# Attention followed by a feed-forward block: output stored by one DMA per token tile, under a new instruction order

## The chip, the cores and the metric

The kernel runs on one core of a Trainium2 chip. Its time is the device time of one execution in microseconds (us); the median of three runs is given. A profile is one further execution, recorded by the hardware profiler.

The core has five instruction streams that run side by side and meet at semaphores: PE (matrix multiplication, its weight loads shown as PEld), DVE (vector), ACT (activation functions), POOL (general purpose, here also the issuer of the loads from device memory) and SP (here only an issuer of DMAs). Each stream runs its own instructions strictly in program order. All DMAs of the core are carried by the same 16 DMA engines.

## The reference

A linear attention with an exponential feature map, and a feed-forward block behind it, without a residual:

```python
# q, k, v: (8 batches, 8 heads, 576 positions, 64); w_phi: (64, 128)
def phi(x):
    proj = einsum('bhsd,df->bhsf', x, w_phi)
    proj = proj - max(abs(proj), axis=-1, keepdims=True)
    return concatenate([exp(proj), exp(-proj)], axis=-1)
q_p, k_p = phi(q), phi(k)
kv = einsum('bhsf,bhsd->bhfd', k_p, v)
z  = sum(k_p, axis=2)
attn = einsum('bhsf,bhfd->bhsd', q_p, kv) / (einsum('bhsf,bhf->bhs', q_p, z) + 1e-6)
x = attn.transpose(0, 2, 1, 3).reshape(4608, 512)       # one row per token
h = maximum(x @ w_in, 0)                                # w_in (512, 2048)
out = (h * h) @ w_out                                   # w_out (2048, 512), float32
```

## The kernel before

The work falls into two halves that are laid over each other. The attention of the eight batches produces rows of x. The feed-forward block consumes them in 36 token tiles of 128 rows, four tiles to a chunk, nine chunks.

**Attention.** POOL issues the loads of k, v and q (line 350), which also turn them to bf16. From batch 2 on, SP issues transposing DMAs of k and q (line 419, tiles kT and qT); the first two batches are transposed by PE (line 430). PE multiplies by w_phi (lines 484, 625, 657), ACT takes exponentials (lines 513, 529, 632), PE forms kv (line 579) and the quotient's parts (line 725), DVE scales them into a tile xo of 128 tokens (line 746). Then xo is transposed into xT, for the later batches by a DMA that SP issues (line 765).

**Feed-forward.** `ffn_in` (line 777) multiplies xT by w_in (line 787), ACT takes the relu (line 792, tile hr), POOL or, from chunk 7 on, DVE squares it (lines 795 and 798, tile h). `ffn_out` (line 807) accumulates one token tile over 16 matmuls of 512 columns (line 818), in four parts of four. After the fourth part DVE copies the sum from PSUM to one of three buffers of 128 x 512 float32, the ring `r_ot` (tile ot, line 835), and SP stores it. A buffer is free again when its store has landed. The very last tile is done in two halves of 256 columns, each copied by its own engine and stored in two pieces, one issued by SP and one by ACT (line 830).

**Where rows lie.** A batch has 576 positions, which is nine blocks of 64 for each of the 64 places that line 804 calls p. So a token tile is two blocks, u = 0 and 1, on partitions 0 to 63 and 64 to 127 of ot. Block j of batch b goes to the rows b\*576 + 9\*p + j, so one block is 64 rows of 2 KB, nine rows apart. The order of the blocks in a batch is `jord` (lines 397 and 398), in pairs j and j + 2. Because nine is odd, four of the 36 tiles (4, 13, 22 and 31) hold the last block of one batch and the first of the next; all others lie in one batch.

**Order.** No scheduler runs in the kernel. Every piece of work is first recorded as an operation with a number, and `Plan.play` then emits the operations in the order of the long list `ORDER` (lines 93 to 184), which was found by a search outside the kernel. A negative number -n stands for n small matmuls that keep PE occupied (line 384). The rings give out their buffers in the order in which `ORDER` takes them. So the list settles the order on every engine and also which of the three ot buffers a tile gets. An SP issue carries a wait for the landing of the DMA that used the same of eight completion semaphores, which is the one eight issues back, beside the wait for its data.

Of the kernel before, what the change touches and what calls it, by code (L numbers as in the profile page):

```python
# [44 lines left out]
class Plan:  # L45
# [48 lines left out]
    7 9 11 6 13 15 17 19 10 1 2 8 4 5 -15 33 34 -3 50 54 51 16 -3 37 38 55 56 35 -1 72 39 52 36 57 59 53 73 74  # L94
    75 41 42 76 81 79 61 65 62 -6 94 40 -4 83 95 77 78 70 66 68 84 87 67 64 63 89 85 -2 43 44 18 -2 45 47 46 48
    -4 116 96 12 21 23 25 14 60 49 86 92 88 90 20 111 118 117 80 82 69 71 -1 100 102 58 91 115 114 97 93 27 29
    22 137 139 98 99 101 104 103 138 107 105 158 160 108 106 132 109 112 119 113 120 121 110 125 126 122 127
    159 133 136 135 134 140 128 153 154 161 157 179 123 129 124 141 142 146 147 130 131 155 156 181 143 144 148
    149 180 150 145 24 26 1465 1461 31 387 174 178 200 177 176 182 175 167 162 168 163 1462 169 164 1468 201
    170 165 171 202 1463 389 1466 1469 1470 1464 1467 166 183 214 215 151 216 188 184 189 152 195 198 199 197  # L100
    196 227 228 203 229 231 1471 185 190 218 186 1477 219 187 204 191 217 192 205 1472 1473 226 232 233 1478
    1474 1475 1476 1479 209 210 172 238 193 173 230 194 242 243 236 237 211 206 207 212 208 213 1480 239 244
    1481 247 1482 245 249 260 253 250 1494 1495 1490 256 257 246 240 1483 1486 241 234 1491 262 261 255 1487
    252 251 28 265 1508 30 220 222 267 221 223 224 225 266 235 1492 248 1489 1493 388 399 390 407 401 405 264
    258 254 259 1509 263 270 287 269 268 288 289 272 271 273 275 274 1510 1484 1496 391 393 1485 392 276 279
    278 303 306 305 277 308 309 310 304 280 281 290 307 32 1497 1501 1502 329 324 331 311 282 285 330 286 284
    283 1516 312 1504 1517 326 328 1505 327 325 332 394 1518 1506 1488 395 397 396 398 313 314 296 317 291 1507
    297 292 293 315 318 1511 316 298 299 300 294 400 1515 319 345 420 346 295 320 321 350 351 1519 301 347 322
    348 302 323 1498 1512 1522 349 1499 1513 1523 421 422 1520 1521 403 352 423 1526 1500 1514 402 371 373 372
    425 366 368 1527 353 1533 1525 354 1549 367 1534 369 1524 565 1535 567 1528 566 569 359 1532 333 427 426  # L110
    355 360 338 1529 1550 429 370 1530 424 428 1551 568 404 406 339 356 340 361 334 335 1539 362 341 363 357
    336 358 435 430 337 1536 374 1537 419 364 1546 365 342 437 436 1540 343 1541 344 438 439 571 1538 570 1531
    573 572 1555 1562 431 432 433 434 1547 1569 415 409 411 412 417 418 410 416 413 414 408 440 462 479 442 441
    443 1576 1577 1556 375 574 577 1548 589 579 583 1557 1573 464 376 380 1559 377 381 463 378 379 382 481 1558
    1542 480 483 482 1574 1560 1563 1564 444 484 383 384 486 485 575 0 1575 465 1561 487 446 447 453 445 506
    448 452 449 450 507 508 457 454 451 501 466 461 460 456 459 1552 1543 488 489 455 494 495 490 1553 458 1544
    576 591 593 509 1554 1579 504 1580 496 472 491 1566 385 492 497 473 498 493 467 474 468 475 476 1570 469
    470 471 503 502 745 1565 1581 747 1567 510 505 1571 386 1603 746 516 511 517 512 748 1503 499 477 580 603
    578 598 605 1585 513 518 514 519 515 520 521 604 1545 1589 1593 1597 1607 597 1572 1568 749 751 523 528 607
    526 524 1611 1615 600 599 601 527 529 530 1598 1616 581 582 478 500 522 1622 1623 1612 550 608 551 552 750  # L120
    752 602 525 1613 606 531 1624 753 1614 1600 1582 1630 609 610 1608 1601 1631 1583 553 755 1584 1632 585 586
    618 620 619 584 613 545 546 547 532 548 611 754 1609 612 1636 549 1637 1602 1610 1638 923 756 1640 1586
    1594 1595 554 1621 1587 1641 1642 1618 533 560 538 1625 590 592 587 1617 595 771 757 588 594 596 614 615
    1619 617 622 1596 925 1620 1588 621 534 539 555 684 1629 556 561 557 540 535 562 685 686 558 541 536 559
    542 1644 1633 563 564 537 1634 1604 1645 616 635 1605 924 662 663 664 636 639 637 638 758 630 631 632 624
    629 634 633 625 657 661 640 642 623 626 660 659 927 641 643 665 658 644 627 628 778 780 779 926 1639 1590
    650 1643 645 1591 666 687 929 928 1606 931 1592 646 651 679 728 730 1648 680 652 647 672 1647 653 729 731
    673 648 649 654 1651 769 1599 543 763 1578 761 775 759 667 674 1652 544 782 688 683 681 682 689 1626 1649
    1627 668 690 694 695 675 676 1675 696 691 669 670 692 671 693 697 698 1628 930 760 762 1679 706 701 783 708
    707 785 784 767 655 1683 705 703 704 702 781 1650 1646 1657 1661 1665 1687 709 710 786 723 726 724 764 788  # L130
    793 1688 1653 765 677 678 656 699 700 1669 794 1670 1676 1708 1694 727 787 1677 725 732 1695 1678 933 1712
    1662 1693 1697 770 776 772 773 774 1709 1710 1713 1663 777 795 789 790 791 792 766 768 820 815 798 822 1701
    821 738 739 800 799 1690 819 818 816 817 932 1103 1671 935 1635 1664 1696 1714 1691 1672 1720 1721 955 934
    953 797 1673 802 716 1666 717 740 741 711 733 718 712 734 1705 713 1706 719 714 735 1684 1658 801 736 742
    737 939 715 720 936 940 1674 1722 1692 1685 796 823 1659 1667 1668 1105 1660 1104 743 949 947 945 721 722
    951 937 1707 943 1689 812 806 842 843 844 804 805 803 808 807 809 810 811 813 837 838 814 840 841 839 956
    966 958 1654 1106 824 3 1655 1656 957 959 845 1107 1686 1109 1702 1680 1711 1715 830 1703 1681 846 968 831
    1719 825 826 832 847 852 848 853 833 967 1698 1704 1682 1699 1700 827 1723 849 854 1716 1717 1718 850 851
    828 855 856 834 1724 1729 970 1108 1733 859 860 908 829 938 1110 864 865 910 866 909 867 1111 1765 1769
    1773 863 862 861 868 969 881 886 887 961 884 885 744 835 857 941 836 858 1737 1741 963 888 1788 869 1744  # L140
    1742 874 1726 882 960 883 1745 1727 1113 889 1728 1738 962 964 875 870 876 1762 1739 1740 1763 911 1764
    1777 877 948 944 946 950 952 954 1020 976 1725 942 878 1021 978 1780 871 872 1022 873 1112 1789 890 1781
    965 1790 1746 1281 1730 1752 1747 1770 1753 1731 1114 1283 1782 1732 1778 977 980 971 903 906 907 972 973
    904 1771 912 1023 1754 1772 896 897 1784 1774 1751 1756 1775 905 974 1757 1758 918 891 892 1766 913 914 919
    1755 898 915 1785 1786 979 975 1767 1119 1117 1115 920 893 921 899 900 916 922 894 917 895 1743 879 1133
    1779 1127 1734 1759 1760 1116 1735 982 993 995 994 998 1000 999 1768 1001 984 981 983 996 1135 1736 1776
    997 1024 985 1002 986 988 990 1086 1087 1015 987 1016 1017 1018 989 1136 880 1783 1787 1791 991 992 1019
    1003 1025 1008 1748 1138 1137 1139 1749 1140 1026 1009 1030 1027 1801 1004 1031 1010 1032 1005 1006 1011
    1033 1028 1012 1007 1118 1795 1792 1793 1282 901 1131 1129 1120 1750 1805 1796 1034 1029 1088 1146 1147
    1042 1141 1142 1143 1044 1148 1013 1035 1121 1125 1123 1761 1809 1819 1823 1794 1827 902 1014 1036 1820  # L150
    1816 1810 1145 1821 1144 1043 1045 1817 1818 1811 1812 1822 1089 1284 1813 1814 1122 1150 1151 1064 1066
    1152 1059 1060 1061 1831 1832 1065 1153 1833 1842 1838 1824 1802 1062 1149 1063 1839 1843 1046 1825 1067
    1840 1285 1844 1826 1286 1124 1081 1085 1156 1037 1083 1038 1039 1041 1084 1068 1803 1040 1090 1157 1158
    1837 1841 1845 1860 1856 1861 1082 1857 1159 1804 1862 1287 1288 1047 1069 1070 1048 1834 1052 1071 1074
# [32 lines left out]
def kernel(  # L187
# [10 lines left out]
    nc = tc.nc  # L198
# [608 lines left out]
    def ffn_out(c, i, key):  # L807
# [25 lines left out]
        elif part == 3:  # L833
# [3 lines left out]
            def fn():  # L837
                for u in range(2):
                    g = 2 * (first[c] + tt) + u
                    nc.sync.dma_start(out=outv[g // NJ, jord[g // NJ % 2][g % NJ]],  # L840
                                      in_=o.t[u * 64 : u * 64 + 64, :])
# [88 lines left out]
```

## Time and profile before

| | before |
|---|---|
| median of 3 runs | 357.59 us (352.43, 357.59, 357.99) |
| the profiled execution | 352.77 us, its span 351.0 us |
| granted PE clock in the profile | 0.994 |
| PE busy | 339.3 us, 97% of the span |
| DVE / ACT / POOL busy | 243.6 / 242.6 / 197.9 us |
| DMA packets of the POOL queue (loads) | 16144, 18.35 MB, 35.3% of 16 engines' time |
| DMA packets of the SP queue (transposes, stores) | 50176, 20.00 MB, 34.5% |
| issues of stores of 128 KB | 70, median 2.4 us from issue to landing |

The span is the time from the first to the last instruction. Busy times are sums for an engine over the span. "SPq" is SP's issuing of DMAs, which is not counted as busy. A DMA's share is the time of its packets divided by the span of 16 engines; packets that overlap on one engine count twice. The three runs lie at two levels, one at 352.4 us and two near 357.8 us; the profiled execution stands with the lower.

### The profile page before, as it was taken

The numbers are of one execution on the slowest core, as the hardware profiler recorded it, in microseconds if no ns is written. First come the engines' busy times: TensorE is split into PE (matmuls) and PEld (weight loads), VectorE is DVE, ScalarE is ACT, GpSimd is POOL, SyncE is SP. The second block draws the span as 40 slices with busy tenths as digits, with TensorE's granted clock in tenths as the row PEclk, the third lists the DMA queues.
The fourth block names the chain that finished last, engine by engine and source line by source line (L and its number), as shares of the span: only waits on it lengthen the run. The fifth ranks groups of instructions, "written<-read, shape, count | busy, mean of one in ns | idle before, by whom it ended". The sixth has DMA issues, their size and how long they took to land.

```text
span 351.0 us, 10160 instructions
## 1 busy us (share of the span) xinstructions
PE 339.3 (97%) x4045; PEld 197.8 (56%) x4045; DVE 243.6 (69%) x553; ACT 242.6 (69%) x496; POOL 197.9 (56%) x305
## 2 busy tenths in 40 slices
PE   6999999998999999999999999998999999999995
PEld 3579877767645654465446544654545544544444
DVE  1999968995887898677867797667468446632531
ACT  3999997988588958895778649946795255703510
POOL 8865976859958672989397619945961020000000
PEclk9899999999999999999999999999999999999999
DMA  7999986998996995949996255793322323021134
GB/s 117 202 210 209 206 119 95 137 190 102 153 156 98 173 175 79 151 56 177 177 120 126 33 83 96 114 163 63 69 43 47 77 48 76 3 45 43 36 87 104
DMA packets 66528, 39.13 MB, mean 111 GB/s; under 512 B 46257, under 2 KB 60977, under 8 KB 66481
## 3 DMA queue, kind: packets, MB, share of 16 engines
q0 software_dynamic: 16144, 18.35, 35.3%
q1 hardware_dynamic: 50176, 20.00, 34.5%
q8 instruction: 31, 0.51, 0.6%
q10 hardware_dynamic: 160, 0.13, 0.2%
q14 instruction: 17, 0.13, 0.1%
HBM read 36.77 MB, written 9.44 MB: 132 GB/s over the span
## 4 chain that ended last, share of the span: by engine, by line
PE 85%; ACT 6%; DMA 4%; DVE 2%; issue 1%; SPq 0%; POOL 0%; DVEq 0%; POOLq 0%
PE one L787 35%; PE one L818 33%; PE one L725 5%; PE one L579 4%; PE one L484 2%; PE one L625 2%; PE one L657 2%; DMA xk<-in_k_dram 2%; ACT qph L632 2%; DMA xT<-xo 1%; ACT kph L529 1%; ACT kph L513 1%; ACT hr L792 1%; DVE mk L495 1%; DMA out_dram<-ot 1%
## 5 line engine op out<-in xcount | busy, mean ns | idle before, releaser
L795 POOL TENSOR_TENSOR h<-hr 128x512 bf16<-128x512 bf16 x112 | 114.3, 1039 | 52.2 <-ACT hr L792 48.1
L787 PE MATMUL one<-xT,win 128*128 128x512 bf16 (+2 forms) x768 | 138.5, 326 | 2.5 <-DVE xo L746 1.2
L818 PE MATMUL one<-wout,h 128*128 128x512 bf16 (+1 forms) x592 | 136.8, 373 | 0.0
L792 ACT ACTIVATE hr<-one 128x512 bf16<-128x512 f32 x144 | 84.7, 616 | 48.5 <-PE one L787 37.3
L787 PEld LDWEIGHTS <-win 128*128 128x128 bf16 x768 | 66.1, 98 | 51.4 <-issue 4.3
L632 ACT ACTIVATE qph<-one 128x512 bf16<-128x512 f32 (+1 forms) x160 | 81.1, 577 | 19.7 <-PE one L625 19.5
L818 PEld LDWEIGHTS <-h 128*128 128x128 bf16 x592 | 54.0, 98 | 56.2 <-issue 1.3
L513 ACT ACTIVATE kph<-ksh 128x1024 bf16<-128x1024 f32 (+1 forms) x66 | 62.1, 969 | 15.8 <-DVE ksh L505 15.7
L495 DVE TENSOR_REDUCE mk<-one 128x4 f32<-128x512 f32 (+1 forms) x80 | 49.6, 627 | 9.7 <-PE one L484 8.1
L687 POOL COPY mq<-m 64x4 f32<-64x4 f32 x108 | 20.0, 185 | 46.6 <-DVE m L678 42.8
L678 DVE TENSOR_REDUCE m<-one 128x4 f32<-128x512 f32 (+1 forms) x60 | 36.0, 630 | 13.9 <-PE one L657 10.4
L735 DVE TENSOR_TENSOR one<-one,em 128x260 f32<-128x260 f32 (+1 forms) x80 | 32.1, 430 | 19.0 <-PE one L725 14.2
L505 DVE TENSOR_TENSOR ksh<-one,mk 128x512 f32<-128x512 f32 (+1 forms) x66 | 41.4, 627 | 4.7 <-ACT kph L513 1.4
L725 PEld LDWEIGHTS <-qph 128*128 128x128 bf16 x640 | 30.9, 97 | 16.8 <-issue 0.9
L835 DVE COPY ot<-one 128x512 f32<-128x512 f32 x35 | 23.9, 684 | 18.5 <-PE one L818 18.3
L725 PE MATMUL one<-kv_sb,qph 128*128 128x65 bf16 x640 | 34.5, 194 | 0.7 <-DVE one L735 0.2
L746 DVE TENSOR_TENSOR xo<-one,rden 128x256 bf16<-128x256 f32 (+1 forms) x80 | 31.3, 416 | 3.7 <-DMA xT<-xo 2.7
L798 DVE TENSOR_TENSOR h<-hr 128x512 bf16<-128x512 bf16 x32 | 12.9, 420 | 13.8 <-ACT hr L792 13.6
L579 PE MATMUL one<-va,kph 64*128 64x65 bf16 x1152 | 21.9, 190 | 0.2 <-DVE ksh L505 0.2
L579 PEld LDWEIGHTS <-kph 64*128 64x128 bf16 x1152 | 20.3, 94 | 2.2 <-DVE mk L495 0.4
L742 DVE RECIPROCAL rden<-one 128x4 f32<-128x4 f32 (+1 forms) x80 | 11.7, 170 | 8.7 <-PE one L725 8.3
L529 ACT ACTIVATE kph<-one 128x512 bf16<-128x512 f32 x28 | 15.9, 620 | 0.6 <-PE one L484 0.5
(46 smaller groups left out, 218.4 us busy)
## 6 DMA issues: line engine op xcount, KB each, us to landing
out_dram<-ot SPq DMA_DIRECT2D x70, 128.0 KB, 2.4
xv<-in_v_dram POOLq DMA_DIRECT2D x14, 288.0 KB, 5.9
xq<-in_q_dram POOLq DMA_DIRECT2D x14, 288.0 KB, 5.0
xk<-in_k_dram POOLq DMA_DIRECT2D x12, 288.0 KB, 5.5
win<-in_moe_w_in_dram POOLq DMA_DIRECT2D x2, 1024.0 KB, 15.5
wout<-in_moe_w_out_dram POOLq DMA_DIRECT2D x2, 1024.0 KB, 18.8
xk<-in_k_dram POOLq DMA_DIRECT2D x1, 576.0 KB, 19.5
xv<-in_v_dram POOLq DMA_DIRECT2D x1, 576.0 KB, 21.1
```

What stands on the lines that cost most here:

```text
L495: nc.vector.tensor_reduce(out=mk.t[:, e, ms], in_=wv(e), axis=AX.X, op=ALU.max, apply_absolute_value=True)
L505: nc.vector.tensor_tensor(out=ksh.t[:, e, : n // 2, :], in0=wv(e), in1=mk.t[:, e, ms].to_broadcast([P, n // 2, Fd]), op=ALU.subtract)
L513: nc.scalar.activation(out=t.t[:, :, : n // 2, :].rearrange("x e i f -> x e (i f)"), in_=ksh.t[:, :, : n // 2, :].rearrange("x e i f -> x ...
L579: nc.tensor.matmul(out=kvp(w, hi)[:, 2 * prl + s], lhsT=kph[g][s].t[r, i % 2, i // 2, :], rhs=va[s if g < nf else 0].t[r, u, : D + 1], sta ...
L632: nc.scalar.activation(out=t.t.rearrange("f (r b) hi p -> f b r hi p", b=2)[:, bk, :, :, lo:hi_], in_=w[bk].t[:, : nj * 256].rearrange("f ...
L678: d1 = [dve(kk, nj * 256, lambda w=w, m0=m0, nj=nj, bk=bk: nc.vector.tensor_reduce(out=m0.t[:, bk, : 2 * nj], in_=w[bk].t[:, : nj * 256].r ...
L725: nc.tensor.matmul(out=w.t[:, z * P : z * P + D + 1], lhsT=qg[s].t[:, h // 2, h % 2, :], rhs=kv[r][0].t[:, z % 2, z // 2, s, :], start=(s ...
L735: nc.vector.tensor_tensor(out=x, in0=x, in1=em.t[lo:hi_, hs].to_broadcast(list(x.shape)), op=ALU.mult)
L787: nc.tensor.matmul(out=w.t[:, y * n : (y + 1) * n], lhsT=win[:, kc, mc * P : (mc + 1) * P], rhs=xT.t[:, a:z, kc, :], start=(kc == 0), stop ...
L792: o = act(key - 4, TCH, lambda: nc.scalar.activation(out=r.t, in_=w.t, func=ACT.Relu), [p_], [w, r])
L795: o = pool(key - 4, 1050, lambda: nc.gpsimd.tensor_tensor(out=t.t, in0=r.t, in1=r.t, op=ALU.mult), [o], [r, t])
L818: nc.tensor.matmul(out=w.t[:, cols], lhsT=h2[c, mc, tt][0].t[:, h2[c, mc, tt][1] :][:, :P], rhs=wout[:, mc, cols], start=(mc == 0), stop=( ...
```

## The change

The store of a token tile whose two blocks lie in one batch is one DMA of 256 KB from all 128 partitions. On the side of the output it has two blocks, 64 rows in each, and 512 numbers in each row. The four tiles across two batches keep their two DMAs of 128 KB, and the very last tile keeps its four of 64 KB. So SP issues 31 large stores, 8 of the former kind and 2 of the last tile's, where it issued 70 and 2. The list `ORDER` is replaced as a whole by another result of the search, made with more time allowed for transfers. The operations in it are the same, but nearly every instruction on PE, ACT, DVE, POOL and SP has other neighbours; there are 44 of the occupying matmul steps for 41.

```diff
 ORDER = """
-    7 9 11 6 13 15 17 19 10 1 2 8 4 5 -15 33 34 -3 50 54 51 16 -3 37 38 55 56 35 -1 72 39 52 36 57 59 53 73 74
+    7 9 1 2 11 6 13 15 8 -15 33 34 4 5 -3 50 54 51 17 19 21 23 10 -3 37 39 38 55 56 40 35 53 36 52 3 72 73 59
...
-    2102 2103 2087 2088 2089 2090 2091 2109 2110 2111 2112 2104 2105 2113 2106 2107 2108
+    2097 2109 2086 2087 2088 2089 2110 2111 2090 2112 2091 2113 2104 2105 2106 2107 2108
 """
...
             o = Buf(r_ot)
             d = dve(key - 2, 560, lambda: nc.vector.tensor_copy(out=o.t, in_=w.t), [p_], [w, out_, o])
 
-            def fn():
-                for u in range(2):
-                    g = 2 * (first[c] + tt) + u
-                    nc.sync.dma_start(out=outv[g // NJ, jord[g // NJ % 2][g % NJ]],
-                                      in_=o.t[u * 64 : u * 64 + 64, :])
+            g = 2 * (first[c] + tt)
+            ab = [(x // NJ, jord[x // NJ % 2][x % NJ]) for x in (g, g + 1)]
+
+            def fn(ab=ab):
+                (b0, j0), (b1, j1) = ab
+                if b0 == b1:
+                    nc.sync.dma_start(out=outv[b0, j0 : j1 + 1 : j1 - j0], in_=o.t)
+                    return
+                for u, (bb, jj) in enumerate(ab):
+                    nc.sync.dma_start(out=outv[bb, jj], in_=o.t[u * 64 : u * 64 + 64, :])
             stores.append(store(key, fn, [d], [o]))
```

In the changed kernel the large store is line 843 and the pair line 846.

## The prediction

> **What bounds the kernel now.** I read the page first, then the waits of PE, the windows by stage, the DMA list and the timeline of the end.
>
> ```profile
> span 351.0 us, 10160 instructions
> PE 339.3 (97%) x4045; PEld 197.8 (56%) x4045; DVE 243.6 (69%) x553; ACT 242.6 (69%) x496; POOL 197.9 (56%) x305
> q0 software_dynamic: 16144, 18.35, 35.3%
> q1 hardware_dynamic: 50176, 20.00, 34.5%
> q8 instruction: 31, 0.51, 0.6%
> PE 85%; ACT 6%; DMA 4%; DVE 2%; issue 1%; SPq 0%; POOL 0%; DVEq 0%; POOLq 0%
> out_dram<-ot SPq DMA_DIRECT2D x70, 128.0 KB, 2.4
> PE one L430 <- DMA xk<-in_k_dram: 1.9, 2, 1.5
> ```
>
> PE is the bound: busy for 339.3 of 351.0 us, so all its idle time is 11.7 us. Its longest wait for a DMA sums to 1.9 us, and no store stands among its waits. The stores land 2.4 us after their issue and nobody in the middle waits for them. The two big DMA queues together use 69.8% of the 16 engines, which is an average; the windows say where it lies:
>
> ```profile
> core 0: us, PE busy (x) PEld busy (x) DVE busy (x) ACT busy (x) POOL busy (x), PEclk, DMA share, GB/s
> 50.00:75.00 25.00, 25.00 (x284) 17.65 (x283) 21.98 (x48) 21.57 (x42) 18.33 (x20) 1.00 1.04 141
> 100.00:125.00 25.00, 24.44 (x353) 13.75 (x351) 19.60 (x43) 22.02 (x46) 19.47 (x33) 1.00 1.08 145
> 250.00:275.00 25.00, 25.00 (x344) 13.82 (x341) 17.27 (x43) 19.05 (x38) 12.87 (x17) 1.00 0.27 55
> ```
>
> The eight windows from 50 to 250 us have DMA shares 1.04, 0.99, 1.08, 0.90, 0.88, 0.67, 0.53 and 0.70. Shares above 1 mean that packets overlap a little on an engine, and that up to 125 us the engines have no room. After 250 us they are nearly empty. The end:
>
> ```profile
> 331.55 13.88 SPq L840 DMA_DIRECT2D out_dram<-ot  x12
> 333.05 14.02 PE L818 MATMUL one<-wout,h 128*128 128x512 bf16 x80
> 343.61 0.69 DVE L835 COPY ot<-one 128x512 f32<-128x512 f32 x1 [1.90 <-PE one L818]
> 347.10 0.37 ACT L826 COPY ot<-one 128x256 f32<-128x256 f32 x1 [12.48 <-DMA out_dram<-ot]
> ```
>
> PE ends at 347.07 us (333.05 + 14.02). The last 3.9 us are a wait for a store to free an ot buffer, a copy, and the last store's landing. Here, and only here, a store is on the path that sets the end.
>
> **The change, part by part.** *Removed: 31 SP issues* at 0.59 us each, 18 us of SPq, which is idle for long stretches between its issues. Worth nothing by itself while PE is the bound; were SP late, it would be worth up to 0.6 us at each transpose behind a store.
>
> *Changed: the way a store is dealt to the engines.* The packet records of the trace show a store of 128 KB as 64 packets of 2 KB and 16 closing words of 4 bytes: four packets on each of 16 engines. Its instruction counts 64 rows first. The built program's listing of the changed kernel has 2x64x512 for the large store's output, two blocks first, where it had 64x512. No DMA in the trace has so small a first count, so the price must be bounded. If the dealing stays as now, each engine gets 8 packets, about 1.2 us at the 150 ns or so that a packet takes in bursts. If it goes by the first count, two engines get 64 packets each and the other 14 none. A 2 KB packet takes from 84 ns (the lowest tenth, and the median in most windows of mixed traffic) to 155 ns (the median in late bursts, all 16 engines storing at once): 64 x 84 = 5.4 us to 64 x 155 = 9.9 us. The page's instruction queue gives a check: 31 packets of 16 KB in 0.6% of 16 x 351 us, 1.1 us each, so 128 KB would be 8.7 us, inside the bounds. I take two engines, since the first count is just what the new pattern changes, and 84 ns, since two storing engines are nearest to the rows with few stores at once.
>
> On this the Trainium skill has a rule, in "DMA: Bandwidth & Descriptors", section "Why a DMA increments its semaphore by 16 and not by 1": a DMA is spread over the largest number of engines, up to 16, that divides the slowest dimension of both sides, here 2 and 128, so two. The trace agrees as far as it goes (64 rows, 16 closing words) and shows no case of 2. The same page's "Rules for kernel authors" speaks both ways: one 128-partition transfer in place of two halves, but a large dimension outermost. Its specification of about 27 GiB/s for an engine would make an estimate of 4.5 us a store, and a span near 364 us.
>
> *The end, by the changed order.* In the listing I counted PE's last matmuls backwards at 0.216 us (512 columns) and 0.108 us (256 columns), and followed DVE's copies and SP's stores. Relative to PE's end, the large stores left are ready at about -21.9, -21.2, at once after these one pair, then one as soon as its buffer is free, then -7.9, -6.2 and one that needs the buffer of the store before last: six large ones. All meet on the same two engines. First packet 1.1 us after issue (at 339.14 us the trace has its first packet 1.12 us later): from -20.7 on, 6 x 5.4 us, 1 us for the pair, is 33.4 us, so the last is through at +12.7. With 1.3 us for closing and the small last pieces the kernel ends 14 us after PE, against 3.9 us now: **+10 us**. At 155 ns it is 6 x 9.9 + 1.2 = 60.6, an end at +41, so +37.
>
> *The middle.* From 50 to 250 us the shares sum to 6.79 x 25 = 170 us an engine. 40 of the 70 stores are issued by then, each 64 packets of 130 ns over 16 engines, 0.52 us: 21 us. The rest, loads and transposes, 149 us, stays. Twenty tiles are 18 large stores and two pairs: 18 x 5.4 + 2 = 99 us. So the two engines get 248 us of packets in 200 us of room. Bounds: 0, if the lead of loads and transposes and their overlap swallow it (PE's waits for DMAs are near nothing now, so some lead exists, of unknown length), and +48, if nothing does. At 155 ns it is 18 x 9.9 + 2 + 149 = 329, up to +129. I take **+20**, somewhat under the middle at 84 ns, since the shares count overlap twice.
>
> *What waits.* Behind a large store on SP's ring of the two engines stand the next transposes (kT, qT, xT land in 4.9, 4.4 and 3.0 us now); a transpose is done only when all its parts are. PE's lines 484, 625, 657 and 787 wait for these. POOL's loads share the two engines packet by packet. A third path is ot: three buffers held some 8 us each where 2.4 us was enough; DVE's copy blocks, and with it all that DVE does for PE. And an SP issue waits for the DMA eight issues back.
>
> *Moved: everything else, by the new list.* Three more keeping matmul steps, next to idle time. A gain is bounded by PE's whole idle time, -11.7 us; for the loss I take the same size, since the waits that it could lengthen are these. I take 0, as neither the head nor the middle shows a removed wait that I could name.
>
> **Sum.** 351.0 + 10 + 20 + 0 = 381 us span; the profiled execution has 1.8 us around its span (352.77), so 383 us. The median of the runs shown, 357.59, lies 4.8 us above the profiled execution and the lowest run 0.3 us below it; I stay near the lower level and say **384 us**.
>
> **Rivals.** *The two engines carry it, at the high price* (packets at 155 ns, little overlap, PE starved through transposes and ot): 351 + 37 + 97 (three quarters of 129) + 2 = 487 us; half way between the prices some 430. For it: the late bursts and the instruction queue's pace. Against it: with two engines storing, the crowd of the late bursts is missing.
>
> *The two engines carry it, but the middle hides it:* 351 + 10 + 2 = 363 us, on the border of what can be told. For it: PE's 1.9 us of waits for DMAs, nothing to do after 250 us. Against it: shares of 1.04 and 1.08 before the change.
>
> *The store is dealt over 16 engines as before:* 1.2 us of packets in place of two times 0.6, hidden as now. The change then does nothing by its stores; with half the order's bounds 352 to 363, likeliest 358 us. For it: every DMA of the trace is dealt over 16. Against it: every one has a large first count.
>
> *The other side, faster:* dealt over 16 and the new order takes out the holds on PE's chain. The place is the chain's one wait for xT at 233.33 us (4.4 us), the wait for the ot buffer at the end (2.3 us) and PE's idle time in the first 50 us (5.0 us): 11.7 us, so 346 us from the median. It decides if transposes get ahead of their matmuls by those few us. Against it: most of the first 50 us waits for loads, which the change doesn't speed.
>
> **How the numbers follow.** Forecast 384 us: 0.60. High price: 0.12. Hidden in the middle: 0.10. Dealt as before: 0.10. Faster: 0.08. A measurement of this kernel can tell about 2% from no change, 350.4 to 364.7 us. The hidden case falls half on each side of that border, so within 2% is 0.10 + 0.04, faster 0.08, slower 0.60 + 0.12 + 0.06 = 0.78. The likeliest case alone reaches from 361 (middle 0) to about 411 us (middle +48). The range has to take in the middle prices above and the cases at the border below: 357 to 432 us, leaving out the faster case and the upper part of the high price.
>
> **What would show it.** Right: a landing time of large stores of 7 us or more, where 2.4 us stands now; SPq waiting for stores; PE idle between 50 and 250 us, released by transposes or by DVE; an end more than 10 us after PE's last matmul. Fewer packets would not show it, as there are 64 for each half either way. Wrong: large stores landing in about 3 us. Then the dealing is as before and what remains is the order. Wrong in size: long landings, but PE busy for nearly as large a share; then the end's +10 alone should be seen.

## The result, and the profile after

The changed kernel takes 405.38 us (median of 4 runs, 399.64 to 409.62), the kernel before, in the same comparison, 355.53 us. The ratio is 1.133, with a 95% interval of 1.108 to 1.158; it leaves out the runs that lie more than 1.5% above the fastest run of their kernel, and so is not 405.38 / 355.53. The profiled execution took 403.63 us.

The page of the changed kernel, with the lines that answer to those shown of before: span, busy times, DMA queues, chain, and the issues of the large stores. It gives no landing time for these.

```profile
span 401.9 us, 10103 instructions
PE 345.5 (86%) x4011; PEld 201.9 (50%) x4048; DVE 244.2 (61%) x553; ACT 244.1 (61%) x496; POOL 199.0 (50%) x305
q1 hardware_dynamic: 49246, 20.00, 47.2%
q0 software_dynamic: 16144, 18.35, 38.2%
PE 71%; DMA 18%; issue 4%; DVE 3%; SPq 2%; ACT 1%; POOL 0%; DVEq 0%; ACTq 0%; POOLq 0%
out_dram<-ot SPq DMA_DIRECT2D x31, 256.0 KB
```

PE now works for 86% of the span, and DMAs hold 18% of the chain that ended last, where they held 4%. The bytes are the same, but the packets of SP's queue stand in their records for 47.2% of a longer span instead of 34.5%. The waits of PE and of the copies, and the windows of the middle (columns as before: busy times, granted PE clock, DMA share, GB/s):

```profile
PE one L787 <- DMA xT<-xo: 11.4, 2, 10.3
PE one L625 <- DMA qT<-xq: 10.9, 1, 10.9
DVE ot L835 <- DMA out_dram<-ot: 16.3, 5, 7.6
ACT ot L826 <- DMA out_dram<-ot: 19.1, 1, 19.1
75.00:100.00 25.00, 13.82 (x253) 9.90 (x252) 9.96 (x20) 12.24 (x26) 7.61 (x19) 0.80 1.42 92
150.00:175.00 25.00, 14.68 (x114) 6.95 (x115) 10.81 (x24) 8.68 (x16) 6.04 (x13) 0.73 1.43 97
250.00:275.00 25.00, 18.99 (x273) 11.24 (x275) 12.05 (x26) 12.76 (x26) 12.55 (x17) 0.86 1.60 105
```

PE, which waited 1.9 us for DMAs before, stands still for 10.9 us for one set of transposes and for 10.3 us for another. In the windows shown, where the long stops lie, all engines idle together. The DMA share is at its highest, 1.42 to 1.60, and yet only 92 to 105 GB/s are moved, where shares of 1.04 and 1.08 moved 141 and 145 GB/s before. This is what few engines with full queues would look like; the records do not name a packet's engine. The timeline of the end:

```profile
374.70 13.15 PE L818 MATMUL one<-wout,h 128*128 128x512 bf16 x75
389.82 0.69 DVE L835 COPY ot<-one 128x512 f32<-128x512 f32 x1 [3.25 <-DMA out_dram<-ot]
395.13 0.37 ACT L826 COPY ot<-one 128x256 f32<-128x256 f32 x1 [19.14 <-DMA out_dram<-ot]
```

PE ends at 387.85 us and the kernel at 401.9: 14.05 us for the stores, where it was 3.9 us.

### The profile page after: what moved, and what is told of

Same layout as the page of the kernel before. It is cut to its first block, busy times and chain, and to the rows that moved or that the text cites. A ratio compares the mean times of both kernels' runs of the same rounds, so it can differ in the third digit from the quotient of the medians.

```text
span 401.9 us, 10103 instructions
## 1 busy us (share of the span) xinstructions
PE 345.5 (86%) x4011; PEld 201.9 (50%) x4048; DVE 244.2 (61%) x553; ACT 244.1 (61%) x496; POOL 199.0 (50%) x305
## 3 DMA queue, kind: packets, MB, share of 16 engines
q1 hardware_dynamic: 49246, 20.00, 47.2%
## 4 chain that ended last, share of the span: by engine, by line
PE 71%; DMA 18%; issue 4%; DVE 3%; SPq 2%; ACT 1%; POOL 0%; DVEq 0%; ACTq 0%; POOLq 0%
PE one L787 28%; PE one L818 25%; DMA xT<-xo 6%; DMA qT<-xq 5%; PE one L579 5%; PE one L725 5%; DMA out_dram<-ot 3%; PE one L657 2%; PE one L625 2%; DMA kT<-xk 2%; PE one L484 2%; DMA xk<-in_k_dram 2%; SPq L419 1%; DVE mk L495 1%; PE one L430 1%
## 5 line engine op out<-in xcount | busy, mean ns | idle before, releaser
L795 POOL TENSOR_TENSOR h<-hr 128x512 bf16<-128x512 bf16 x112 | 114.7, 1040 | 88.9 <-ACT hr L792 83.4
L787 PE MATMUL one<-xT,win 128*128 128x512 bf16 (+2 forms) x768 | 141.4, 331 | 16.2 <-DMA xT<-xo 11.4
L818 PE MATMUL one<-wout,h 128*128 128x512 bf16 (+1 forms) x555 | 135.2, 377 | 2.9 <-issue 1.4
L792 ACT ACTIVATE hr<-one 128x512 bf16<-128x512 f32 x144 | 83.4, 606 | 73.4 <-PE one L787 57.9
L818 PEld LDWEIGHTS <-h 128*128 128x128 bf16 x592 | 54.1, 98 | 56.4 <-issue 3.5
L725 PEld LDWEIGHTS <-qph 128*128 128x128 bf16 x640 | 32.4, 99 | 19.1 <-issue 2.3
L725 PE MATMUL one<-kv_sb,qph 128*128 128x65 bf16 x640 | 36.1, 196 | 0.2 <-ACT qph L632 0.2
L579 PE MATMUL one<-va,kph 64*128 64x65 bf16 x1152 | 23.2, 194 | 5.0 <-issue 5.0
L579 PEld LDWEIGHTS <-kph 64*128 64x128 bf16 x1152 | 21.6, 97 | 6.4 <-issue 5.9
L625 PE MATMUL one<-qT,wphi 64*128 64x256 bf16 (+1 forms) x160 | 14.6, 266 | 11.1 <-DMA qT<-xq 10.9
L484 PE MATMUL one<-wphi,kT 64*128 64x128 bf16 x288 | 14.4, 227 | 3.0 <-DMA kT<-xk 1.6
```

Of the source, the lines that this page charges most:

```text
L579: nc.tensor.matmul(out=kvp(w, hi)[:, 2 * prl + s], lhsT=kph[g][s].t[r, i % 2, i // 2, :], rhs=va[s if g < nf else 0].t[r, u, : D + 1], sta ...
L725: nc.tensor.matmul(out=w.t[:, z * P : z * P + D + 1], lhsT=qg[s].t[:, h // 2, h % 2, :], rhs=kv[r][0].t[:, z % 2, z // 2, s, :], start=(s ...
L787: nc.tensor.matmul(out=w.t[:, y * n : (y + 1) * n], lhsT=win[:, kc, mc * P : (mc + 1) * P], rhs=xT.t[:, a:z, kc, :], start=(kc == 0), stop ...
L792: o = act(key - 4, TCH, lambda: nc.scalar.activation(out=r.t, in_=w.t, func=ACT.Relu), [p_], [w, r])
L795: o = pool(key - 4, 1050, lambda: nc.gpsimd.tensor_tensor(out=t.t, in0=r.t, in1=r.t, op=ALU.mult), [o], [r, t])
L818: nc.tensor.matmul(out=w.t[:, cols], lhsT=h2[c, mc, tt][0].t[:, h2[c, mc, tt][1] :][:, :P], rhs=wout[:, mc, cols], start=(mc == 0), stop=( ...
```

## The experiments

Each ratio is against the kernel before, run beside it on the same chip. The median of the kernel before was between 351.2 and 355.5 us in these comparisons, so a difference of a few us between kernels of different experiments means little. The indented texts are what was expected before each run.

**The order alone.** The old store under the new list.

```diff
-                if b0 == b1:
-                    nc.sync.dma_start(out=outv[b0, j0 : j1 + 1 : j1 - j0], in_=o.t)
-                    return
                 for u, (bb, jj) in enumerate(ab):
```

> The new order with two stores of 128 KB for every tile, as before. If the dealing of the large stores over two engines is the cause, the time falls back to that of the kernel before, 350 to 362 us, PE idle about 7 us in the profile. If the order is the cause, it stays at 395 us or more. If each does part, it lies between, 365 to 390 us.

352.62 us, ratio 1.0023 (0.9984 to 1.0062), span 350.3 us with PE busy for 339.2. Beside pairs of stores the new order changes nothing that can be measured. So the cost comes with the large stores.

**The large stores alone.** The changed kernel with the old list.

```diff
-ORDER = (the list of after)
+ORDER = (the list of before)
```

> The large stores under the order of before, whose transposes have had less time. If two engines carry them, at least as slow as the changed kernel: 400 to 440 us, transposes waited for by PE. If the new order is the cause, 350 to 362 us.

430.55 us, ratio 1.2206 (1.2155 to 1.2258). The new list, worth nothing with pairs, saves 25 us with large stores (430.55 against 405.38): of the 77.5 us that they cost under the old one (430.55 - 353.02) that is a third. That the longer time for transfers is what helps is likely, but no run shows which part of the list does it.

**End and middle apart.** Large stores only in the last two chunks, or only in the first seven.

```diff
-                if b0 == b1:
+                if b0 == b1 and c >= 7:      # the other kernel: c < 7
```

> The new order, large stores only in the last two chunks of eight tiles, pairs in the first seven. If the cost at the end is a backlog of six large stores on two engines, 10 us more than with the new order and pairs alone, nearly all of it after PE's last matmul; PE idle stays near 7 us. If the stores cost only through transposes and loads that meet them, no more than 3 us.

> The new order, large stores in the first seven chunks, pairs in the last two. If end and middle are two terms of a sum, about 40 us more than with the new order and pairs alone, PE idle some 41 us, and an end within 5 us of PE's last matmul. If the delays of the middle are made good by an emptier end, 20 us more or less.

At the end alone: 362.75 us, 10.1 above the order alone, ratio 1.0308 (1.024 to 1.0376). In the middle alone: 393.41 us, 40.8 above, ratio 1.1103 (1.1009 to 1.1197). The two excesses add up to 50.9 us; the changed kernel lies 52.8 us above the order alone. So, within the few us by which comparisons differ, the cost is a sum of two terms. In the profile of the first, the chain that ended last waits for one line only:

```profile
333.77 6.06 PE one L818 x28
340.57 13.48 DMA out_dram<-ot
354.15 0.37 ACT ot L826
```

In the profile of the second, PE ends at 387.5 us (374.35 + 13.15) and the span at 391.6, as short an end as before.

**The same large store with another first count.** The relu writes its tokens interleaved, so that partition 2p + u holds token p of block u, and the store names the 64 places first.

```diff
-            out=r.t, in_=w.t, func=ACT.Relu), [p_], [w, r])
+            out=r.t.rearrange("x (b p u) -> x b u p", p=64, u=2),
+            in_=w.t.rearrange("x (b u p) -> x b u p", u=2, p=64), func=ACT.Relu), [p_], [w, r])
...
-                    nc.sync.dma_start(out=outv[b0, j0 : j1 + 1 : j1 - j0], in_=o.t)
+                    nc.sync.dma_start(
+                        out=outv[b0, j0 : j1 + 1 : j1 - j0].rearrange("j p n -> p j n"), in_=o.t)
```

> The new order with one large store for each tile, but with the place in the block ahead of the block: the output's first count is 64 and not 2. For that the relu writes its 128 tokens of a tile interleaved, so that partition 2p + u holds token p of block u. If the first count deals the store out, each of 16 engines gets 8 packets, a store lands in about 3 us, and the time is that of the new order with pairs, 350 to 362 us. If a store of 256 KB is slow for its size, it stays near 405 us. If the interleaved write costs ACT, its lines at the relu are longer than 616 ns and the time is some us above.

> The same stores with 64 first under the order of before. If a store of one issue in place of two brings anything by itself, 345 to 352 us; if SP's issuing time is hidden, as the prediction had it, within 2% of the kernel before.

Under the new order 353.68 us, ratio 1.0111 (1.0053 to 1.017); under the old one 356.64 us, ratio 1.0166 (1.0085 to 1.0248). The page of the first has the landing and the relu:

```profile
out_dram<-ot SPq DMA_DIRECT2D x31, 256.0 KB, 2.7
L792 ACT ACTIVATE hr<-one 128x512 bf16<-128x512 f32 x144 | 104.2, 769 | 49.1 <-PE one L787 36.1
```

The same 256 KB, in one DMA from 128 partitions, land in 2.7 us. In the store, only the order of two counts in the output's pattern differs from the changed kernel. So neither the size nor the merging is slow. No gain from the single issue is seen: both kernels are 1 to 2% behind before. ACT, with 20.8 us more in the relu (104.2 against 83.4 in the order alone), may be why, and may hide a small gain.

**The interleaving by PE.** The same stores, with PE reading xT's columns in that order and the relu as it was.

```diff
-                        lhsT=win[:, kc, mc * P : (mc + 1) * P], rhs=xT.t[:, a:z, kc, :],
+                        lhsT=win[:, kc, mc * P : (mc + 1) * P],
+                        rhs=xT.t[:, a:z, kc, :].rearrange("x t (u p) -> x t p u", u=2),
```

> The new order with large stores, place ahead of block so that the first count is 64, and the interleaving done by PE, which reads the columns of xT in that order; the relu writes as in the changed kernel. If the 0.16 us that each relu took longer with its interleaved write is what the earlier try of these stores lost, 348 to 353 us, level with the kernel before or up to 1% faster. If a store of one issue brings nothing, no clear difference from before. If PE reads the strided columns more slowly, line 787 is longer than 326 ns in the mean and the time is 360 us or more.

503.24 us, ratio 1.4294 (1.423 to 1.4359). Line 787 went from a median of 379 ns to 644 ns. The stores landed in 2.5 us, but this way costs far more than it could save, so whether ACT was the reason for the 1% stays open.

**Pairs with small first counts.** The old pair of stores, its rows named with a first count of 2 or 4.

```diff
-            out=r.t, in_=w.t, func=ACT.Relu), [p_], [w, r])
+            out=r.t.rearrange("x (b l h) -> x b h l", b=8, l=2),       # the other kernel: l=4
+            in_=w.t.rearrange("x (b h l) -> x b h l", b=8, l=2), func=ACT.Relu), [p_], [w, r])
...
-                    nc.sync.dma_start(out=outv[g // NJ, jord[g // NJ % 2][g % NJ]],
+                    nc.sync.dma_start(out=outv[g // NJ, jord[g // NJ % 2][g % NJ]].rearrange("(h l) n -> l h n", l=2),
```

> The new order with pairs of 128 KB, as many issues as in the new order alone, but the rows of each store are named with a first count of 2 (the relu writes a block's tokens in the order that this needs). If the first count deals a store to two engines, each tile puts 64 packets on each of two engines as with the large stores, and the time is 395 to 420 us. If the size of one DMA or the merging is the cause, 350 to 362 us.

> The same with a first count of 4: four engines, 32 packets a tile on each, 2.7 to 3.1 us. By the sum of the prediction these four have 149 us of loads and transposes and 20 x 2.7 = 54 us of stores by 250 us, so 203 us in 200: 353 to 366 us. If anything under 16 engines is as slow as two, 395 us or more.

595.34 and 557.55 us. Both expectations failed, because the relu's new write order made ACT the bound. Its line in the first of the two:

```profile
L792 ACT ACTIVATE hr<-one 128x512 bf16<-128x512 f32 x144 | 344.0, 2612 | 41.0 <-PE one L787 23.4
```

2612 ns instead of 605: the times say nothing about stores. The packet records do. In the kernel before, SP's queue writes 16 closing words of 4 bytes for a plain DMA, and 32 for a transpose: with pairs 74 x 16 + 87 x 32 = 3968, which is what the trace has. With first count 2 there are 2960, with 4 there are 3104: exactly 2 and 4 words for each of 72 stores. And the 128 packets of a pair on quiet queues take 6.3 us with a first count of 2 and 3.5 us with 4, though each store has 128 KB as before. So a small first count slows a store without any merging. The changed kernel has 3038, which is 31 x 2 + 12 x 16 + 87 x 32, and the rows-first kernel 3472, with 31 x 16.

**Half the columns.** The time of the two engines halved.

```diff
-                    nc.sync.dma_start(out=outv[b0, j0 : j1 + 1 : j1 - j0], in_=o.t)
+                    nc.sync.dma_start(out=outv[b0, j0 : j1 + 1 : j1 - j0, :, :256], in_=o.t[:, :256])
```

> The changed kernel, with only the first 256 of 512 columns of each large store written (the other half of those rows is left out): 64 packets on each of two engines, of 1 KB. At 46 to 75 ns a packet that is 3 to 4.8 us a store for about 6.2. If the time of the two engines is the cause, the cost falls by more than half, to 360 to 380 us, as it is their overload and not their use that costs; if it is the number of packets, it stays near 405 us.

361.72 us, ratio 1.0318 (1.0203 to 1.0433): 10.5 us above the kernel before of its comparison (351.24), where full rows cost 49.9 (405.38 - 355.53). The other half of the rows stays unwritten. The packets took 46 ns in the median, and their number is the same. So it is not the number of packets, but the time on the two engines, and the cost is that of an overload: about half the time costs about a fifth.

**Six buffers.**

```diff
-    r_ot = ring("ot", 3, [P, DM], F32)
+    r_ot = ring("ot", 6, [P, DM], F32)
```

> The changed kernel with six ot buffers for three. If DVE's wait for an ot buffer is what stops the middle, 375 us or less. If the transposes and loads behind the stores on two engines stop it, 395 us or more: DVE's wait for stores goes (16 us in the profile), but PE's idle time stays near 40 us.

406.34 us, ratio 1.1591 (1.1544 to 1.1638). DVE no longer waits for a store, and PE waits the more for transposes:

```profile
PE one L625 <- DMA qT<-xq: 24.2, 2, 12.5
```

The third path of the prediction, the buffers, is not what stops the middle.

**Another ring.** The large stores issued by ACT.

```diff
-                    nc.sync.dma_start(out=outv[b0, j0 : j1 + 1 : j1 - j0], in_=o.t)
+                    nc.scalar.dma_start(out=outv[b0, j0 : j1 + 1 : j1 - j0], in_=o.t)
```

> The changed kernel with the large stores issued by ACT in place of SP, at the same place of the order. They run on the same two engines but not ahead of the transposes on SP's ring. If the transposes suffer from standing behind a store in one ring, the time falls to 365 to 385 us, less what ACT's waits for DVE's copies cost. If it is the two engines' time, however it is shared, it stays at 395 us or more.

Two runs, 403.14 and 409.75 us, where the changed kernel's lie between 399.64 and 409.62; that is too few for a ratio. PE still waits 17.9 us for xT. This speaks for the two engines' time against the place in one ring, but does not settle it, as ACT's stream now also waits for DVE's copies, and ACT's own copies for stores.

## Why the prediction was right, and where its sum was short

The direction and the mechanism held; the forecast was 384 us and the result 405.

*The dealing.* Right. The records don't name the engine of a packet; that there are two is read from the closing words (2 for each large store) and from the pace (in a backlog 128 packets of 84 ns in 5.0 us, two at a time). That the first count decides is shown by the same store with 64 first. The rule of the Trainium skill ("DMA: Bandwidth & Descriptors", section "Why a DMA increments its semaphore by 16 and not by 1") that the slowest dimension of both sides sets the number of engines agrees with the counts of 2, 4 and 16 words. The advice in its "Rules for kernel authors" for one transfer of 128 partitions in place of two halves, taken alone, points the wrong way here: the output's first count decided.

*The price.* Close. An undisturbed large store takes 6.2 us from its first to its last packet, 97 ns a packet, between the ends of 84 and 155. With the 1.15 us from issue to first packet it lands after some 7.5 us, the sign of 7 us or more that the prediction named. In the backlog of the end one takes 5.0 us, so there 84 ns was the right value or a little high. The high price did not occur. The prediction's other estimate, 4.5 us a store, was below both. With the forecast's share of the middle (20 of 48) it would have made 351 + 5 + 13 = 369 us, and not the 364 that is named there.

*The end, +10.* Right: 14.05 - 3.9 = 10.1 us in the profiles, and 10.1 us by the kernel with large stores at the end alone. This was no luck: in the packet records the last six large stores and the pair run one behind the other from 20.9 us before PE's end to 12.3 us after it, where the forecast had 20.7 before and 12.7 after.

*The middle, +20.* This is the step that failed, in size. It measured 40.8 us by the kernel with large stores in the middle alone. The working had 248 us of packets for 200 us of room, and then took less than half of the +48 because of overlap and lead. These helped less than that, and the sum had no term for PE's clock. Against the order alone, PE's idle time rose from 11.1 us (350.3 - 339.2) to 56.4 (401.9 - 345.5), 10 of it at the end, so some 35 us in the middle. Two stops, of 10.9 us for qT and 10.3 us for xT, are more than half of it; two more, of 4.8 and 4.0 us, have no cause in the profile.

Why the lead did not last is only in part shown. The transposes landed later. These are the landings of kT, in the order alone and then with large stores in the middle alone:

```profile
kT<-xk SPq DMA_TRANSPOSE x30, 5.3
```

```profile
kT<-xk SPq DMA_TRANSPOSE x30, 10.3
```

And SP issued them more slowly, which the prediction had only as a queue behind a wait. The groups of transposes by line 419, of the order alone and then of the changed kernel (minimum, median and maximum duration of the issue):

```profile
L419 SPq DMA_TRANSPOSE kT<-xk x30: 1189/1265/2346, 45.3 to 237.0; - x30
```

```profile
L419 SPq DMA_TRANSPOSE kT<-xk x30: 1167/1984/9583, 45.7 to 278.1; - x30
```

In the changed kernel the issue of a transpose behind a large store lasts up to 9.6 us, and SP issues nothing else meanwhile. This alone hardly explains the time: with the large stores on ACT's ring the issues of kT are nearly as short as in the order alone (1.27 us in the median, at most 3.0), and the time is that of the changed kernel. There ACT's own waits may have put other costs in its place, so how much of the middle each of the two delays costs stays open.

*What was left out: the clock.* PE's busy time grew by 6.3 us (345.5 - 339.2) with the same work. That may be too little, as 37 of the 592 matmul records of line 818 are missing from this profile. With large stores in the middle alone none is missing; the order alone and this kernel have:

```profile
PE 339.2 (97%) x4048; PEld 197.9 (56%) x4048; DVE 243.1 (69%) x553; ACT 243.4 (69%) x496; POOL 198.5 (57%) x305
PE 352.7 (90%) x4048; PEld 202.5 (52%) x4048; DVE 243.8 (62%) x553; ACT 244.0 (62%) x496; POOL 198.7 (51%) x305
```

So of the 41 us of the middle 13.5 are slower work (352.7 - 339.2) and 27.8 are idle time (38.9 - 11.1). In the changed kernel's windows with the long stops the granted clock is 0.80, 0.73 and 0.86, where every window of the middle had 1.00 before. The clock's records have half speed in stretches of 3.4, 6.8, 10.2 and 13.7 us that begin in a stop and outlast it. This agrees with "TensorE: Matmul & The Clock Gate", section "Part 1: The HAM clock gate", by which an idle window of about 3.4 us halves the clock until a busy one has passed. As to the length the runs do not quite agree: with large stores at the end alone, a stop of only 2.0 us, after small matmuls of line 579, was followed by 3.4 us at half speed.

*The order, 0.* Right by itself (1.0023), but not independent of the stores, as the sum had it: with large stores the two lists differ by 25 us.

*The rivals.* "Hidden in the middle" fell with 40.8 us. "Dealt as before" would have been the rows-first kernel, and that is 1 to 2% slower. This also speaks against "faster": even dealt over 16 engines, one issue in place of two showed no gain, though the dearer relu of these kernels could hide a small one. No kernel tried is faster than before.

## What to carry to other kernels

Before two stores are merged into one, look at the first count of the pattern on each side, since a count of two can put a transfer on two of 16 engines. Then sum the packets that these engines get beside everything else, stage by stage, and don't discount an overload by much for overlap or lead. Here the middle cost 41 us where the packets exceeded the room by 48: transposes land later, the stream that issues is held up, and PE's stops cost clock speed as well. In a trace the sign is a high DMA share with few GB/s, and for a plain store the closing words (2, 4 and 16 here) go with the count of engines.

## What the runs showed of the hardware that was not expected

The relu's write order mattered far more than thought. Contiguous it takes 605 ns; in long runs of 64 with a step of 4 bytes 769 ns; in runs of 2 or 4 with steps of 64 or 32 bytes 2612 and 2485 ns. Whether the short runs or the steps are dear wasn't separated. PE, reading its moving columns in runs of two, 128 bytes apart, needs 644 ns in place of 379 (medians of line 787). An issue of a transpose on SP, 1.27 us in the median and at most 2.3 us (kT) in the order alone, lasts up to 9.6 us in the changed kernel.
